# Output products on TensorE's row tiles, key work on its column tiles, and one pool of PSUM slots

## The chip, the cores and the metric

The kernel runs on one core of a Trainium2 chip. The metric is the device time of one execution in microseconds (us). Before the change three runs took 443.28, 443.36 and 443.82 us; the median is 443.36.

A core has five engines that work side by side, each through its own queue in order: TensorE (PE, matrix products into PSUM), VectorE (DVE), ScalarE (ACT), GpSimd (POOL) and SyncE (SP, which here only issues transfers). PSUM is the memory that TensorE writes; it has eight banks of 512 float32 columns by 128 partitions.

## The reference

Four batches of 12544 queries go through attention with 49 agents, and the result through a maxout network. With `sm` the softmax over the last axis of the scaled products:

```python
a2k = sm(agents, k)            # 49 x 12544 per batch
agent_v = a2k @ v              # 49 x 128
q2a = sm(q, agents)            # 12544 x 49
x = (q2a @ agent_v).reshape(50176, 128)
h = np.maximum(np.maximum(x @ w1, x @ w2), x @ w3)   # 768 wide
out = h @ w_out                # 50176 x 128, float32
```

## The kernel before

**The rearrangement.** x is never formed. For each batch the kernel multiplies agent_v with the weights once, into a small table G (49 rows used, in both halves of the partitions): its columns hold agent_v times w3-w1, times w2-w1, and times w1 times w_out. With e the exponentials of a query's 49 scores, the maximum over three becomes w1's part plus max(0 or u, v), where u comes from w3-w1 and v from w2-w1. So the output is e times G's linear part plus r times w_out, r being the maximum, all divided by the sum of e at the end.

**Blocks.** The queries are cut into 49 blocks `s` of 1024 (eight tiles of 128); block 48 takes the last 256 queries of each of the four batches. For each block:

- `ql`, `qc`: load by SP, cast to bf16 on POOL. Then the transpose: for 29 blocks by a transfer (`qd`), for 20 on TensorE (`qt`, L531) with a copy on DVE (`qe`, L535).
- `sc` (L541): scores, two matmuls of 512 columns, on column tiles (one gives partitions 0 to 63, the other 64 to 127). `ex` (L547): exponential on ACT. `su` (L553): four small matmuls for the sums; `re` (L558): reciprocals on DVE.
- For six slices `f` of the 768 hidden columns: `u` and `v` (L566), each a pair of matmuls with 49 rows and 512 columns, one on the upper, one on the lower 64 rows of the array (row tiles, which run side by side) into two banks. `a` (L579): ACT writes max(0, u); `x` (L582): DVE takes the maximum of that and v into r. For slice 4, v is added to u in place and ACT does both steps (L573, L576).
- In two halves of four query tiles, `o.s.0` and `o.s.1`: `li` (L595), the linear part with two matmuls of 256 columns each, then for each slice `p` (L604), four matmuls of 128 rows, 128 columns with r as the weights. `ov` (L611): DVE scales by the reciprocals. `st`: SP stores the block.

**Keys.** Batch 0's keys and values are worked through first, in 12 chunks (from 0 to about 39 us). Those of batches 1 to 3, in 11 chunks each, are spread over blocks 1 to 34: `ks` (scores, L367), `kx` (exponential), `kv` (values, L384), each nine small matmuls on the whole array with a host block's sums in the same PSUM tile; `va` on DVE and `ea` on POOL add up. When a batch is done, `gpa`, `gpc` and `gpl` make its G.

**Array modes.** A matmul runs on the whole array (full), on 64-row tiles (row) or on 64-column tiles (column). u and v are row, the query scores and G's products are column, all else is full.

**PSUM.** Three slots of two banks (`UV`) hold u, v and the products; two slots of one bank (`OM`) hold scores, sums and keys, transposed queries and the output halves: eight banks. `SLOTS` gives the counts.

**The order.** `graph` lists all operations with their engine and data; the costs, modes and service times it passes are not used when the kernel runs. The string `ORDER` then gives one sequence of all operations, with the slot of each new tile behind a slash; `Emit.run` issues them in it, and so each engine's queue has the order of its own operations in the string. An operation waits by semaphore for its data and for its slot's last reader.

Of the kernel before, what the change touches and what calls it, by code (L numbers as in the profile page):

```python
# [9 lines left out]
FP32 = mybir.dt.float32  # L10
# [7 lines left out]
DFF = NF * P  # L18
SCALE = 1.0 / math.sqrt(C)
C31, C21, C1O, WC = 0, DFF, 2 * DFF, 2 * DFF + 2 * C  # L20
# [11 lines left out]
SLOTS = {"UV": 3, "OM": 2, "LD": 13, "QB": 3, "KB": 3, "VB": 4, "KT": 3, "QT": 3, "EQ": 4, "EK": 4, "AS": 3,  # L32
         "R": 13, "RC": 4, "OS": 11, "G": 4, "VA": 2, "EA": 2, "ES": 2, "KR": 2}
SHAPE = {"UV": ([P, 2, 512], FP32), "OM": ([P, 512], FP32), "LD": ([P, KT, C], FP32), "QB": ([P, GT, C], BF16),
# [6 lines left out]
class Plan:  # L41
# [5 lines left out]
    def add(self, name, eng, fn, cost, mode=FULL, after=(), new=(), use=(), bank=None, serve=0.0):  # L47
# [4 lines left out]
        seq = [self.maker[t] for t in use if self.maker[t] not in after]  # L52
        self.ops.append(dict(name=name, eng=eng, fn=fn, pace=cost[0], lat=cost[1], mode=mode, after=list(after), seq=seq,
                             new=[t for _, t in new], use=[t for _, t in new] + list(use), bank=bank, serve=serve))
# [61 lines left out]
def graph(plan, em):  # L116
# [5 lines left out]
    for g, (t0, n) in enumerate(ch):  # L122
# [4 lines left out]
        add(f"kt0.{g}", PE, em.k_turn(g, n), mm(n, 128), after=[f"kc0.{g}", "prep"], new=[("UV", f"kT_ps0.{g}")], use=[f"kb0.{g}"])  # L127
        add(f"ke0.{g}", DVE, em.k_evacuate(g, n), dve_half(n * 128), after=[f"kt0.{g}"], new=[("KT", f"kT0.{g}")], use=[f"kT_ps0.{g}"])
        add(f"ks0.{g}", PE, em.k_scores(0, g, n, f"s0.{g}"), mm(n, 49), after=[f"ke0.{g}"], new=[("UV", f"s0.{g}")], use=[f"kT0.{g}"])
        add(f"kx0.{g}", ACT, em.k_exps(0, g, n, f"s0.{g}"), (n * 0.041 + 0.07, n * 0.041 + 0.2), after=[f"ks0.{g}"],  # L130
            new=[("EK", f"e0.{g}")], use=[f"s0.{g}"])
        add(f"to0.{g}", PE, em.totals(g, n), mm(1, n * 49), after=[f"kx0.{g}"], new=[("OM", "acc")] if g == 0 else [],
# [9 lines left out]
    for g in range(SPARE):  # L142
        add(f"wm.{g}", PE, em.warm(g), (0.2225, 0.45), new=[("OM" if g == 0 else "UV", f"warm.{g}")])
# [12 lines left out]
    add("tw1", PE, em.turn_w1, mm(NF, 128), after=["cw1", "prep"], new=[("OM", "tw1")])  # L156
# [6 lines left out]
    for name, c, d, eng in (("a", C31, ["d31a"], ACT), ("b", C31 + half, ["d31b", "d32"], DVE), ("c", C21, ["d21a"], ACT),  # L163
                            ("d", C21 + half, ["d21b"], DVE)):
        add(f"gp{name}", PE, em.product(0, c, c + half, f"gp{name}"), mm(1, half), mode=COL, after=["nr0"] + d, new=[("UV", f"gp{name}")])
        add(f"gv{name}", eng, em.product_out(0, c, c + half, c, f"gp{name}", eng), act(half) if eng == ACT else dve(half),
            after=[f"gp{name}"], use=[f"gp{name}", "G0"])
    add("pl", PE, em.prep_linear, mm(NF, 128), after=["ew1", "cwo"], new=[("OM", "pl")])
    add("el", ACT, em.evacuate_linear, (0.17, 0.31), after=["pl"], use=["pl"])
    add("gl", PE, em.product(0, C1O, WC, "gl"), mm(1, 256), mode=COL, after=["nr0", "el"], new=[("OM", "gl")])  # L170
# [713 lines left out]
```

## Time and profile before

| | |
|---|---|
| median of three runs | 443.36 us |
| span of the profiled execution, first to last instruction | 440.9 us |
| time of the profiled execution beyond its span | not in the page; the median is 2.46 us above the span |
| TensorE busy | 421.0 us (95%), 5246 matmuls |
| DVE busy | 390.6 us (89%) |
| ACT busy | 392.4 us (89%) |
| POOL busy | 169.3 us (38%) |
| u and v matmuls, L566 | 1248, 182.6 us busy |
| output matmuls, L604 to OM | 2340, 178.3 us busy |
| TensorE clock | 0.999 of full speed |

A group line gives: line, engine, operation, tiles out and in with their shapes, the count; busy time and the mean length of one in ns; then the engine's idle time just before these instructions and what ended it. A timeline line gives start, length, engine, line, operation and count of a merged run of equal instructions; PEld is TensorE loading weights. Matmuls overlap and their ends are modelled, so the spacing of starts says more than busy time. A window line gives the stretch, its length, then each engine's busy time with its count, the granted clock, the mean busy share of the 16 DMA engines and GB/s.

### The profile page before, as it was taken

How to read it: one execution, taken by the hardware profiler on the slowest of the kernel's cores; microseconds unless marked ns; L12 is line 12 of the kernel's file. 1: busy time of each engine (PE TensorE's matmuls, PEld its weight loads, DVE VectorE, ACT ScalarE, POOL GpSimd, SP SyncE). 2: the span in 40 equal slices, each digit the busy share in tenths (PEclk: the TensorE clock that was granted, in tenths of full speed). 3: DMA queues.
4: the chain of work that ended last, by engine and by line, in shares of the span. 5: the costliest groups of instructions: out<-in, count | busy, mean ns of one | idle time of the engine just before them, and what ended most of it. 6: DMA issues, size and time to landing. Idle time of an engine off the chain costs nothing.

```text
span 440.9 us, 12824 instructions
## 1 busy us (share of the span) xinstructions
PE 421.0 (95%) x5246; PEld 268.6 (61%) x5246; DVE 390.6 (89%) x495; ACT 392.4 (89%) x461; POOL 169.3 (38%) x176
## 2 busy tenths in 40 slices
PE   2678999999999999999999999999999999999997
PEld 2564565666666665666666666665665655656676
DVE  2236998999999999999999989989999999999996
ACT  2269999999998999999999999999999999999983
POOL 3541556667295413480746345634403102000000
PEclk9999999999999999999999999999999999999999
DMA  8999999999999999999999999999987952462144
GB/s 323 409 410 384 347 297 335 315 390 266 399 352 239 297 316 352 273 279 307 419 410 259 242 279 381 268 290 304 277 253 214 246 138 76 117 207 58 49 165 173
DMA packets 99157, 122.50 MB, mean 278 GB/s; under 512 B 72535, under 2 KB 75291, under 8 KB 99099
## 3 DMA queue, kind: packets, MB, share of 16 engines
q1 hardware_dynamic: 98752, 121.46, 92.2%
q8 instruction: 41, 0.67, 0.6%
q10 hardware_dynamic: 347, 0.23, 0.2%
q14 instruction: 17, 0.14, 0.1%
HBM read 78.74 MB, written 25.69 MB: 237 GB/s over the span
## 4 chain that ended last, share of the span: by engine, by line
PE 74%; DMA 15%; ACT 3%; POOL 3%; SPq 2%; DVE 1%; issue 1%; DVEq 0%; ACTq 0%; POOLq 0%
PE UV L566 31%; PE OM L604 28%; DMA LD<-in_k_dram 8%; PE OM L595 5%; PE OM L541 3%; DMA LD<-in_q_dram 2%; ACT AS L579 2%; DMA LD<-in_moe_w_dram 2%; DMA LD<-in_v_dram 2%; PE OM L384 2%; PE OM L531 2%; PE OM L367 2%; DMA KT<-KB 1%; SPq L333 1%; POOL KB L343 1%
## 5 line engine op out<-in xcount | busy, mean ns | idle before, releaser
L582 DVE TENSOR_TENSOR R<-UV,AS 128x1024 bf16<-128x1024 f32 x245 | 293.1, 1218 | 17.2 <-PE UV L566 13.2
L579 ACT ACTIVATE AS<-UV 128x1024 bf16<-128x1024 f32 x245 | 246.1, 1025 | 16.9 <-PE UV L566 13.3
L566 PE MATMUL UV<-EQ,G 49*128 49x512 bf16 (+1 forms) x1248 | 182.6, 369 | 1.0 <-DVE G L456 0.2
L604 PE MATMUL OM<-wo_bf,R 128*128 128x128 bf16 x2340 | 178.3, 220 | 0.0
L604 PEld LDWEIGHTS <-R 128*128 128x128 bf16 x2352 | 139.3, 98 | 41.1 <-issue 38.6
L566 PEld LDWEIGHTS <-G 49*128 49x128 bf16 x1248 | 60.4, 93 | 63.6 <-issue 23.3
L525 POOL CAST QB<-LD 128x1024 bf16<-128x1024 f32 x49 | 50.6, 1043 | 113.4 <-DMA LD<-in_q_dram 73.5
L611 DVE TENSOR_TENSOR OS<-OM,RC 128x512 f32<-128x512 f32 x98 | 66.8, 681 | 3.0 <-PE OM L604 2.0
L343 POOL CAST KB<-LD 128x1152 bf16<-128x1152 f32 (+2 forms) x45 | 50.0, 1120 | 48.7 <-DMA LD<-in_k_dram 32.0
L573 ACT ACTIVATE UV<-UV 128x1024 f32<-128x1024 f32 x49 | 49.9, 1018 | 2.6 <-PE UV L566 1.6
L576 ACT ACTIVATE R<-UV 128x1024 bf16<-128x1024 f32 x49 | 50.2, 1024 | 1.4 <-PE UV L566 0.6
L343 POOL CAST VB<-LD 128x1152 bf16<-128x1152 f32 (+1 forms) x33 | 37.5, 1141 | 26.2 <-PE OM L553 13.6
L595 PE MATMUL OM<-G,EQ 128*128 128x256 bf16 x195 | 37.8, 275 | 0.0
L482 POOL TENSOR_TENSOR EA<-EA,EK 128x441 f32<-128x441 f32 x27 | 27.7, 1026 | 19.1 <-ACT EK L373 18.4
L547 ACT ACTIVATE EQ<-OM 128x512 bf16<-128x512 f32 x49 | 29.5, 603 | 1.2 <-PE OM L541 1.1
L355 DVE COPY KT<-UV 128x1152 bf16<-128x1152 bf16 (+1 forms) x12 | 8.3, 701 | 15.8 <-PE UV L350 13.5
L595 PEld LDWEIGHTS <-EQ 128*128 128x128 bf16 x196 | 12.3, 97 | 15.7 <-issue 15.2
L341 ACT ACTIVATE VB<-LD 128x1152 bf16<-128x1152 f32 (+1 forms) x12 | 12.3, 1040 | 9.9 <-DMA LD<-in_v_dram 9.6
L367 PEld LDWEIGHTS <-KT 128*128 128x128 bf16 x392 | 14.6, 98 | 9.1 <-issue 5.1
L541 PE MATMUL OM<-QT,agT 128*64 128x512 bf16 (+1 forms) x104 | 19.9, 388 | 0.0
L384 PEld LDWEIGHTS <-VB 128*128 128x128 bf16 x392 | 14.0, 96 | 7.3 <-issue 5.6
L373 ACT ACTIVATE EK<-OM 128x441 bf16<-128x441 f32 (+1 forms) x33 | 18.0, 546 | 0.4 <-PE OM L553 0.3
(71 smaller groups left out, 193.3 us busy)
## 6 DMA issues: line engine op xcount, KB each, us to landing
LD<-in_q_dram SPq DMA_DIRECT2D x48, 512.0 KB, 6.8
out_dram<-OS SPq DMA_DIRECT2D x48, 512.0 KB, 5.1
LD<-in_k_dram SPq DMA_DIRECT2D x40, 576.0 KB, 8.3
LD<-in_v_dram SPq DMA_DIRECT2D x40, 576.0 KB, 9.7
LD<-in_v_dram SPq DMA_DIRECT2D x3, 512.0 KB, 8.0
LD<-in_k_dram SPq DMA_DIRECT2D x3, 512.0 KB, 11.2
LD<-in_moe_w_dram SPq DMA_DIRECT2D x6, 192.0 KB, 8.6
KT<-KB SPq DMA_TRANSPOSE x33, 6.6
```

The costliest lines, as they stand in the source:

```text
L343: (self.nc.gpsimd if eng == POOL else self.nc.vector).tensor_copy(out=out, in_=src)
L525: return lambda: self.nc.gpsimd.tensor_copy(out=self.t[f"qb.{s}"], in_=self.t[f"q.{s}"][:, :GT, :])
L541: self.nc.tensor.matmul(self.t[f"qs.{s}"][h * H:(h + 1) * H, jj * P:(jj + pairs) * P], self.agT[:, b, :], self.t[f"qT.{s}"][:, 2 * jj + h: ...
L547: return lambda: self.nc.scalar.activation(self.t[f"e.{s}"], self.t[f"qs.{s}"], AF.Exp, scale=SCALE)
L566: self.nc.tensor.matmul(t[:, h, jj * P:(jj + pairs) * P], self.t[f"G{b}"][h * H:h * H + A, c + f * P:c + (f + 1) * P], self.t[f"e.{s}"][h ...
L573: return lambda: self.nc.scalar.activation(self.t[f"u.{s}.{f}"], self.t[f"u.{s}.{f}"], AF.Relu)
L576: return lambda: self.nc.scalar.activation(self.t[f"r.{s}.{f}"], self.t[f"u.{s}.{f}"], AF.Relu)
L579: return lambda: self.nc.scalar.activation(self.t[f"a.{s}.{f}"], self.t[f"u.{s}.{f}"], AF.Relu)
L582: return lambda: self.nc.vector.tensor_tensor(out=self.t[f"r.{s}.{f}"], in0=self.t[f"v.{s}.{f}"], in1=self.t[f"a.{s}.{f}"], op=ALU.max)
L595: self.nc.tensor.matmul(out[:, c:c + 2 * C], self.t[f"e.{s}"][:, j // 2 * P:(j // 2 + 1) * P], self.t[f"G{of[j // 2]}"][:, C1O:C1O + 2 * C ...
L604: self.nc.tensor.matmul(out[:, c:c + C], self.t[f"r.{s}.{f}"][:, j % 2, j // 2 * P:(j // 2 + 1) * P], self.wo_bf[:, f, :], start=False, st ...
L611: self.nc.vector.tensor_tensor(out=self.t[f"os.{s}"][:, j:j + n, :], in0=self.flat(f"o.{s}.{o}")[:, :n * C].rearrange("p (j c) -> p j c", ...
```

## The change

- **Output products.** A block's output is one tile `o` of two banks (bank 0 for the first four query tiles, bank 1 for the last four) in place of two halves. Each slice's product is split over the 128 rows of r and w_out: `p` takes, for each of four positions, rows 0 to 63 into bank 0 and rows 64 to 127 into bank 1, as a row-tile pair; `y` takes the other rows for each bank. So the two row tiles never add to one bank within a step, but p and y use the banks the other way round. Where the order goes from one side to the other on an unfinished `o`, `turns` marks the operation and a TensorE drain is issued ahead of it.
- **The linear step** is four row-tile pairs of 128 columns; G's linear part is 128 columns wide instead of 256.
- **The transposes on TensorE** are eight row-tile pairs of 64 columns, and the DVE copy reads and writes them in runs of 64.
- **Keys of batches 1 to 3 and all sums** run on column tiles: each matmul of 128 weight columns becomes a pair of 64.
- **PSUM.** One pool `PP` of four slots of two banks holds everything. A block's scores (bank 0) and its sums with the hosted keys (bank 1) share one tile `ax`.
- **The scaling** is one DVE operation of 1024 columns, in the last block two times two of 256. The last block's store cuts the tile as slices of query tiles four apart.
- **The order** is new for all operations.

```diff
-SLOTS = {"UV": 3, "OM": 2, "LD": 13, "QB": 3, "KB": 3, "VB": 4, "KT": 3, "QT": 3, "EQ": 4, "EK": 4, "AS": 3,
+SLOTS = {"PP": 4, "LD": 13, "QB": 3, "KB": 3, "VB": 4, "KT": 3, "QT": 3, "EQ": 4, "EK": 4, "AS": 3,
          "R": 13, "RC": 4, "OS": 11, "G": 4, "VA": 2, "EA": 2, "ES": 2, "KR": 2}
...
+    def turns(self, order):
+
+        turned, side = set(), {}
+        for n in order:
+            o = self.ops[self.index[n]]
+            if o["side"]:
+                t = o["new"][0] if o["new"] else o["use"][-1]
+                if side.get(t, o["side"]) != o["side"]:
+                    turned.add(n)
+                    side = {}
+                side[t] = o["side"]
+        return turned
...
+            if name in turned:
+                self.nc.tensor.drain()
             o["fn"]()
...
+    def later_scores(self, b, g, n, m):
+        def fn():
+            t = self.keys(b, m)
+            for j in range(n):
+                for h, r in self.halves():
+                    self.mm(t[r, j * A:(j + 1) * A], self.t[f"kT{b}.{g}"][:, j, r], self.agT[:, b, :A], start=(j == 0), stop=True)
+        return fn
...
     def q_turn(self, s):
         def fn():
-            t = self.half(f"qT_ps.{s}")
+            t = self.t[f"qT_ps.{s}"].bitcast(BF16)
             for j in range(GT):
-                self.nc.tensor.transpose(t[:, j * P:(j + 1) * P], self.t[f"qb.{s}"][:, j, :], self.ident)
+                for h, r in self.halves():
+                    self.nc.tensor.transpose(t[:, h, j * H:(j + 1) * H], self.t[f"qb.{s}"][r, j, :], self.ident[r, r])
         return fn
...
+            t, e = self.t[f"ax.{s}"], self.t[f"e.{s}"]
             for jj in range(GT // 2):
-                c = CS + 2 * jj
-                self.nc.tensor.matmul(self.t[m][:, c:c + 2], self.t[f"e.{s}"][:, jj * P:(jj + 1) * P], self.sel,
-                                      start=(first and jj == 0), stop=True, skip_group_check=True)
...
+                for h, r in self.halves():
+                    self.mm(t[r, 1, CS + 2 * jj:CS + 2 * jj + 2], e[:, jj * P + h * H:jj * P + (h + 1) * H], self.sel, start=(lone and jj == 0),
+                            stop=True)
+        return fn
...
+    def out_linear(self, s):
         def fn():
             of = [p[0] for p in parts_of(s) for _ in range(p[4])]
...
+            for jj in range(GT // 2):
+                x = slice(jj * P, (jj + 1) * P)
+                for h in range(2):
+                    r = slice(h * H, h * H + A)
+                    self.mm(self.t[f"o.{s}"][:, h, x], self.t[f"e.{s}"][r, x], self.t[f"G{of[jj]}"][r, C1O:WC], start=(jj == 0), stop=False)
+        return fn
+
+    def out_hidden(self, s, f, side):
+
+        def fn():
+            for jj in range(GT // 2):
+                x = slice(jj * P, (jj + 1) * P)
+                for h, r in self.halves():
+                    i = h if side == 1 else 1 - h
+                    self.mm(self.t[f"o.{s}"][:, i, x], self.t[f"r.{s}.{f}"][r, i, x], self.wo_bf[r, f, :], start=False, stop=True)
+        return fn
+
+    def out_scale(self, s):
+        return lambda: self.nc.vector.tensor_tensor(
+            out=self.t[f"os.{s}"], in0=self.flat(f"o.{s}").rearrange("p (j c) -> p j c", c=C),
+            in1=self.t[f"rc.{s}"].unsqueeze(2).to_broadcast([P, GT, C]), op=ALU.mult)
```

Two blocks of the order, before and after, around the output products (a word is an operation, the number behind the slash its slot):

```diff
-p.40.0.2 ov.40.0/4 v.41.4 x.41.4/0 qc.48/0
-v.41.5/1 u.42.1/0 a.42.1/2 x.41.5/6 sc.43/1 ex.43/0 li.40.1/0 p.40.1.4 v.42.0/2 x.42.0/10 p.40.1.0 u.41.3/1 a.41.3/1 v.42.1/0
...
+re.41/2 x.40.2/4 v.40.5/3 u.41.0/0 a.41.0/1 x.40.5/7 li.40/1 p.40.3 p.40.1
+u.41.2/2 a.41.2/2 p.40.0 v.41.0/0 x.41.0/8 p.40.2 qc.44/2 qd.44/0 p.40.4 u.41.1/3 a.41.1/0 p.40.5 u.41.4/2 a.41.4 y.40.2 y.40.0
+v.41.1/0 x.41.1/2 u.41.3/3 a.41.3/1 y.40.1 y.40.5 y.40.3 y.40.4 ov.40/1
...
```

More of the change, by code (lines that the diff above doesn't have):

```diff
@@ L45, in __init__, with add @@
         self.ops, self.index, self.tiles, self.maker = [], {}, {}, {}
-    def add(self, name, eng, fn, cost, mode=FULL, after=(), new=(), use=(), bank=None, serve=0.0):
+    def add(self, name, eng, fn, cost, mode=FULL, after=(), new=(), use=(), bank=None, serve=0.0, side=0):
         self.index[name] = len(self.ops)
@@ L51, in add, with close @@
             self.maker[t] = name
-        seq = [self.maker[t] for t in use if self.maker[t] not in after]
-        self.ops.append(dict(name=name, eng=eng, fn=fn, pace=cost[0], lat=cost[1], mode=mode, after=list(after), seq=seq,
-                             new=[t for _, t in new], use=[t for _, t in new] + list(use), bank=bank, serve=serve))
+        self.ops.append(dict(name=name, eng=eng, fn=fn, pace=cost[0], lat=cost[1], mode=mode, after=list(after),
+                             new=[t for _, t in new], use=[t for _, t in new] + list(use), bank=bank, serve=serve, side=side))
+    def close(self):
+        for o in self.ops:
+            o["seq"] = [self.maker[t] for t in o["use"] if t not in o["new"] and self.maker[t] not in o["after"]]
+    def turns(self, order):
[9 more added lines that the diff above has]
+        return turned
     def places(self, order, given):
@@ L650 @@
     graph(plan, em)
+    plan.close()
     order, given = [], {}
```

630 lines of the change are left out of this document (303 added, 327 removed).

## The prediction

> **What bounds the kernel now.** I read the page first, then the windows, the waits, and last TensorE's timeline, where single groups of matmuls can be timed against each other.
>
> ```profile
> span 440.9 us, 12824 instructions
> ...
> PE 421.0 (95%) x5246; PEld 268.6 (61%) x5246; DVE 390.6 (89%) x495; ACT 392.4 (89%) x461; POOL 169.3 (38%) x176
> ...
> PE 74%; DMA 15%; ACT 3%; POOL 3%; SPq 2%; DVE 1%; issue 1%; DVEq 0%; ACTq 0%; POOLq 0%
> ...
> L582 DVE TENSOR_TENSOR R<-UV,AS 128x1024 bf16<-128x1024 f32 x245 | 293.1, 1218 | 17.2 <-PE UV L566 13.2
> ...
> L604 PE MATMUL OM<-wo_bf,R 128*128 128x128 bf16 x2340 | 178.3, 220 | 0.0
> L604 PEld LDWEIGHTS <-R 128*128 128x128 bf16 x2352 | 139.3, 98 | 41.1 <-issue 38.6
> ```
>
> The runs' median, 443.36, is 2.46 us above this span; I take that as what lies around the span, and every change below as a change of the span. The chain is TensorE's (74%), and L604 has no idle before it at all. From 39 us on, where the blocks start:
>
> ```profile
> core 0: us, PE busy (x) PEld busy (x) DVE busy (x) ACT busy (x) POOL busy (x), PEclk, DMA share, GB/s
> 39.00:441.00 402.00, 397.21 (x4915) 250.81 (x4913) 377.85 (x463) 373.81 (x435) 155.02 (x157) 1.00 0.93 268
> ```
>
> Per block of 49 that is 8.2 us, with DVE idle 24 us and ACT 28 us in total. They mostly wait for TensorE, briefly:
>
> ```profile
> ACT AS L579 <- PE UV L566: 13.3, 42, 0.6
> DVE R L582 <- PE UV L566: 13.2, 35, 0.7
> ```
>
> So TensorE bounds, with two engines close behind. What fills it is seen in starts, not in the modelled ends:
>
> ```profile
> 249.73 0.60 PE L566 MATMUL UV<-EQ,G 49*128 49x512 bf16 x4
> 250.26 0.84 PE L604 MATMUL OM<-wo_bf,R 128*128 128x128 bf16 x12
> 250.94 0.38 PE L595 MATMUL OM<-G,EQ 128*128 128x256 bf16 x2
> 251.25 0.60 PE L566 MATMUL UV<-EQ,G 49*128 49x512 bf16 x4
> 251.79 0.40 PE L604 MATMUL OM<-wo_bf,R 128*128 128x128 bf16 x4
> ...
> 387.92 0.61 PE L566 MATMUL UV<-EQ,G 49*128 49x512 bf16 x4
> 388.46 0.41 PE L541 MATMUL OM<-QT,agT 128*64 128x512 bf16 x2
> 388.80 0.39 PE L566 MATMUL UV<-EQ,G 49*128 49x512 bf16 x2
> ```
>
> Twelve full-array matmuls take 250.26 to 250.94: 0.68, or 0.057 each. Two row-tile pairs of 512 columns record 0.60 and one pair 0.39, so a pair takes 0.215; yet from 249.73 the next form starts after 0.53, not 0.43. The 0.10 is a change of array mode, row tiles to full. Back, 250.94 to 251.25, two 256-column matmuls (0.107 each by the same pace) leave 0.10 again. Into and out of column tiles it is 0.11 (387.92 to 388.46) and 0.12 (388.46 to 388.80).
>
> **The change: modes.** Going along the order's TensorE operations with their modes, I count 592 changes before: 480 between row and full, 70 between row and column, 42 between full and column. At 0.10, 0.115 and 0.10 that is 60 us. After it are 234: 219 row to column or back, 15 with full-array work, all in the start. That is 26.7 us. Gain 33.5 us.
>
> **Output products.** One p step of four 128x128 matmuls becomes p and y, each four pairs of 64-row halves. The nearest row is the last block, which already runs 128-column row-tile pairs with new weights each:
>
> ```profile
> 432.05 0.84 PE L566 MATMUL UV<-EQ,G 49*128 49x128 bf16 x24
> 432.82 1.07 PE L604 MATMUL OM<-wo_bf,R 128*128 128x128 bf16 x16
> 433.82 0.64 PE L566 MATMUL UV<-EQ,G 49*128 49x128 bf16 x16
> ```
>
> Twelve pairs take 0.77 less a mode change of 0.10: 0.056 a pair, as the full matmul. So 48 pairs for 48 matmuls a block, no cost. The linear step drops from four 256-column matmuls (0.43) to four pairs (0.224): 49 x 0.205 = 10 us gained. [...]
>
> **Drains.** The order gives 105: each time p and y alternate on an unfinished o. No row shows one. It can hardly cost less than a mode change, 0.10; from above, a 128-column matmul's record outlasts its pace by 0.220 - 0.057 = 0.163, and a load nobody hides adds 0.098: 0.26. I take the middle, 0.18, being nearest to waiting out the record: 18.9 us (10.5 to 27.3).
>
> **Column tiles and query transposes.** Nearest rows: narrow full-array matmuls, the full-array transposes, and the last block's column pairs.
>
> ```profile
> 30.84 0.63 PE L384 MATMUL OM<-EK,VB 128*128 128x49 bf16 x18
> 31.31 0.38 PE L367 MATMUL UV<-agT,KT 128*128 128x49 bf16 x9
> ...
> 232.18 0.62 PE L531 MATMUL OM<-ident,QB 128*128 128x128 bf16 x8
> 232.63 0.61 PE L604 MATMUL OM<-wo_bf,R 128*128 128x128 bf16 x8
> ...
> 420.24 0.41 PE L541 MATMUL OM<-QT,agT 128*64 128x128 bf16 x8
> 420.59 0.64 PE L566 MATMUL UV<-EQ,G 49*128 49x512 bf16 x4
> ...
> L566 PEld LDWEIGHTS <-G 49*128 49x128 bf16 x1248 | 60.4, 93 | 63.6 <-issue 23.3 <-DVE G L456 0.4 <-DVE R L582 0.2
> ...
> L541 PEld LDWEIGHTS <-agT 128*64 128x64 bf16 x104 | 5.8, 106 | 9.1 <-issue 6.3 <-DMA out_dram<-OS 0.3
> ```
>
> A narrow full matmul takes 0.47/18 = 0.026; a column pair with new weights at most (0.35 - 0.12)/4 = 0.057, and that row streams 128 columns, so it is a ceiling. I take 0.040, midway. Keys: 33 chunks x 2 steps x 9 pairs x (0.040 - 0.025) = 8.9 us (0 to 18.7). Sums: 49 x (4 x 0.040 - 0.10) = 2.9 us (0 to 6.2). The 20 transposes of query blocks: 0.45 each before, eight pairs of 64 columns after, 0.20 to 0.45; at 0.25 they gain 4 us (0 to 5). [...]
>
> **TensorE's sum:** -33.5 - 10 - 4 + 18.9 + 8.9 + 2.9 = -16.8 us. All best ends: -38; all worst: +8.7.
>
> **What is late next.** DVE:
>
> ```profile
> 382.54 2.36 DVE L582 TENSOR_TENSOR R<-UV,AS 128x1024 bf16<-128x1024 f32 x2 [0.30 <-PE UV L566]
> ...
> 388.03 0.69 DVE L611 TENSOR_TENSOR OS<-OM,RC 128x512 f32<-128x512 f32 x1
> 388.64 5.02 DVE L582 TENSOR_TENSOR R<-UV,AS 128x1024 bf16<-128x1024 f32 x4
> ```
>
> A maximum takes 2.36 - 1.22 = 1.14, an output scaling of 512 columns 0.61. One scaling of 1024 at a maximum's pace saves 0.08 a block, 4 us: 374 us of work in the 402. But the pool is smaller: u and v had three slots of their own; now four serve u, v, a whole o (held from the linear step through twelve steps and the 1.14 scaling) and ax (scores to sums and keys). In 33 places, against 9, the next DVE operation reads a product that can only start in the slot this operation frees, 17 of them x.s.0, v.s.1, x.s.1. Each leaves DVE idle for a TensorE round trip; the 0.39 of a pair's record with a little queueing makes 0.5: 16 us. 374 + 16 = 390, 12 us under 402. That is less gain than TensorE's 16.8, so DVE decides: 443.4 - 12 = **431 us**. ACT (373.81) stays behind. SP keeps its 260 issues (loads, transposes, stores) and POOL its 161 operations; only their order moves, and they run ahead of TensorE. Each drain holds everything queued behind it on TensorE, the next u and v among it, so ACT and DVE feel it too once they are the bound. The 20 copies of transposed queries now write runs of 64 columns:
>
> ```profile
> L535 DVE COPY QT<-OM 128x1024 bf16<-128x1024 bf16 x20 | 13.6, 682 | 3.4 <-PE OM L531 3.4
> ```
>
> I take their time as unchanged, since the runs stay long; at the pace of a float maximum they would take 20 x (1.22 - 0.68) = 11 us more on DVE. In the last block two half scalings in four instructions follow the last product where one of 0.42 did: +0.9, against some 1.5 us of TensorE work no longer after the last maximum; nothing net. The first blocks wait for the same 31 loads as before: nothing.
>
> **Rivals.**
> 1. The round trips hide and TensorE's cheaper ends hold: DVE's 374 alone bounds, 443.4 - 28 + a few waits = 420. For it: DVE's other waits were short (0.4). Against: three engines within a few per cent. 0.10.
> 2. Slower by the pool. Of PSUM tiles that follow a DVE or ACT reader, 140 of 694 now wait for the latest instruction listed on that engine, before 58 of 792; those with two or more to spare fall from 290 to 63. At each extra one TensorE can wait up to an instruction, 1.0 to 1.2. It decides from 16.8/82 = 0.2 us a place; at 0.25, 447; at 0.4, 459. Against it: TensorE would then have time to wait. 0.27, of which slower 0.19.
> 3. Drains and column loads at their upper ends: +8.7, 452. 0.15, slower 0.12.
> 4. The halves do not run at 0.056 over long bursts: the x24 row is only 48 instructions with their loads, and TensorE now gets twice the output matmuls. If loads were not overlapped the pair would take the load's 0.098: 49 x 48 x 0.042 = 99 us, 525. [...] Against: that row. 0.04.
> 5. Transfers hold the middle back:
>
> ```profile
> POOL QB L525 <- DMA LD<-in_q_dram: 73.5, 13, 18.9
> ...
> 20.00:40.00 20.00, 16.24 (x256) 11.85 (x254) 8.48 (x17) 14.94 (x21) 5.50 (x5) 1.00 1.03 401
> ...
> 240.00:320.00 80.00, 79.83 (x1016) 50.75 (x1012) 74.13 (x94) 77.02 (x91) 38.38 (x40) 1.00 1.12 291
> ```
>
> The share is as high at 240 to 320 as in the load-bound start. Then only the last 12 blocks gain, 0.25 each: 440. Against: TensorE waits for none of it now. 0.06.
>
> **How the numbers follow.** Forecast 431 (own range 424 to 440): 0.38. Faster: 0.38 + 0.10 + 0.05 (rival 2 mild) + 0.02 (3) + 0.05 (5) = 0.60. Slower: 0.19 + 0.12 + 0.04 = 0.35. Within 0.2%, what a measurement here can tell from no change: 0.05. The range 418 to 455 leaves out rival 4 and the tails of 1, 2 and 3, some 0.15.
>
> **What would show it.** Right: p and y pairs 0.056 apart; mode changes only around column work; gaps of about 0.18 between p and y; key groups of nine pairs lasting 0.36; DVE idle growing around v.s.1 with TensorE idle no longer zero. Wrong: TensorE waits on slots of tenths of a us at most acquisitions, drains over 0.3, output pairs slower than 0.06, or DMA waits ahead of key scores.

## The result, and the profile after

The changed kernel takes 512.25 us (median; 510.32 to 512.82 in four runs) against 443.32 before: a ratio of 1.155, with a 95% interval of 1.1525 to 1.1573. The prediction said 431, with a range up to 455. Both the sign and the size were wrong. Single runs of kernels of after's kind differ by up to 2.5%, the longer ones mostly with a lower mean clock (in e14 below 476.48 us at 0.945 and 488.13 at 0.923); where that matters the range is given.

The page of after answers to the lines shown of before: span, busy times, the granted clock in tenths over 40 slices, the instruction queue (packets, MB, share), the chain, then the costliest groups (busy, mean ns of one, idle before and what ended it).

```profile
span 511.0 us, 19885 instructions
...
PE 430.3 (84%) x8738; PEld 285.9 (56%) x8738; DVE 390.4 (76%) x447; ACT 399.3 (78%) x461; POOL 169.7 (33%) x176
...
PEclk9976799979799999899999999997988999999999
...
q8 instruction: 68, 1.11, 0.9%
...
PE 11%; DVE 5%; ACT 2%; issue 2%; DMA 1%; SPq 0%; DVEq 0%; ACTq 0%
...
L620 DVE TENSOR_TENSOR R<-PP,AS 128x1024 bf16<-128x1024 f32 x245 | 292.8, 1217 | 59.5 <-PE PP L336 49.2
L617 ACT ACTIVATE AS<-PP 128x1024 bf16<-128x1024 f32 x245 | 245.5, 1025 | 56.4 <-PE PP L336 50.2
L336 PE MATMUL PP<-EQ,G 49*128 49x512 bf16 (+1 forms) x1248 | 216.8, 384 | 14.8 <-DVE OS L644 3.5
L336 PE MATMUL PP<-wo_bf,R 64*128 64x128 bf16 x4704 | 205.2, 220 | 15.0 <-issue 4.8
```

All three main engines got idler: TensorE's share fell from 95% to 84%, DVE's and ACT's from 89% to 76 and 78%. DVE's and ACT's idle is a wait for TensorE (49.2 and 50.2 us, before 13.2 and 13.3). So TensorE still sets the pace, and it stands still more. The chain was followed back for 21% of the span only, so it does not help here. The clock, flat before, has dips, and the instruction queue carried 68 packets (of 16 KB each) where before it carried 41. The two lines of before:

```profile
PEclk9999999999999999999999999999999999999999
...
q8 instruction: 41, 0.67, 0.6%
```

The same stretch as in the prediction, from 39 us to the end:

```profile
39.00:511.00 472.00, 406.96 (x8427) 268.97 (x8422) 379.83 (x420) 382.47 (x438) 155.55 (x157) 0.95 0.82 229
```

**What TensorE's time went on.** I booked each gap from one matmul's start to the next: first the streaming at the paces of the prediction's rows (0.056 for 128 columns, 0.215 for 512), then up to 0.11 at a change of mode, up to 0.26 at a drain, the extra streaming time where the granted clock is 0.5, a rest over 0.4 us where the next matmul waits for no semaphore ("stall"), and what is left as a wait. In us, from 39 us to the last matmul of the profiled execution, for before, after and six of the experiments below (in brackets their labels). Each column is one execution. Behind before they took 512.8, 504.0, 503.3, 523.7, 498.9, 466.5 and 492.1 us, which is not always near the median of the kernel's runs:

| | before | after | key scores first (e1) | no drains (e2) | full-array products (e3) | ACT and DVE halved (e5) | halved, three edits (e13) | other order (e11) |
|---|---|---|---|---|---|---|---|---|
| streaming and rests under 0.05 | 331 | 322 | 321 | 320 | 322 | 321 | 321 | 323 |
| mode changes | 58 | 24 | 23 | 24 | 86 | 23 | 23 | 24 |
| drains | 0 | 26.5 | 26 | 0 | 0 | 26.5 | 0 | 21 |
| semaphore waits | 9 | 56 | 50 | 67 | 50 | 42 | 30 | 46 |
| stalls without a semaphore | 0 | 19 | 17 | 14 | 3 | 22 | 29 | 20 |
| half clock | 0 | 19 | 20 | 31 | 15 | 17 | 17 | 11 |
| sum | 398 | 466 | 457 | 456 | 477 | 452 | 419 | 445 |

The first three rows are the work that the prediction summed for TensorE: -8.8, -34.6 and +26.5, together -17. It had said -16.8. The loss is in the other three, which were 9 us before and are 94 after.

Rows of TensorE's timeline show each kind:

```profile
70.23 0.41 PE L336 MATMUL PP<-QT,agT 128*64 128x512 bf16 x2
71.33 0.47 PE L336 MATMUL PP<-agT,KT 128*64 128x49 bf16 x18 [0.69 <-ACT EQ L582]
71.73 0.60 PE L336 MATMUL PP<-EQ,G 49*128 49x512 bf16 x4
...
100.24 0.46 PE L336 MATMUL PP<-agT,KT 128*64 128x49 bf16 x17
101.89 0.21 PE L336 MATMUL PP<-agT,KT 128*64 128x49 bf16 x1 [1.18 <-issue]
...
129.18 0.39 PE L564 MATMUL PP<-ident,QB 64*128 64x64 bf16 x15
131.74 0.19 PE L564 MATMUL PP<-ident,QB 64*128 64x64 bf16 x1 [2.16 <-issue]
131.74 0.40 PE L336 MATMUL PP<-EQ,G 49*128 49x512 bf16 x2
131.97 0.40 PE L336 MATMUL PP<-wo_bf,R 64*128 64x128 bf16 x8
132.19 0.39 PE L336 MATMUL PP<-EQ,G 49*128 49x512 bf16 x2
...
240.32 0.62 PE L336 MATMUL PP<-wo_bf,R 64*128 64x128 bf16 x16
240.78 0.81 PE L336 MATMUL PP<-EQ,G 49*128 49x512 bf16 x6
...
400.62 0.88 PE L336 MATMUL PP<-wo_bf,R 64*128 64x128 bf16 x16
401.33 0.60 PE L336 MATMUL PP<-EQ,G 49*128 49x512 bf16 x4
```

- **The pairs.** Four pairs from 131.97 to 132.19 are 0.22: 0.056 a pair, as predicted.
- **A drain** holds TensorE's next instruction back until the work ahead of it has ended (in e4 below the next load starts 0.08 us behind the last matmul's record). Eight pairs without one take 240.32 to 240.78, 0.46; with one, 400.62 to 401.33, 0.71. A drain costs 0.25 there.
- **The shared tile.** At 71.33 the key scores wait for the exponential of ACT, though it reads bank 0 of the tile `ax` and they write bank 1: here the wait goes by tile, not by bank. In 14 of the 33 chunks the order puts key scores behind that exponential.
- **A stall.** The sixteenth of 16 query transposes starts 2.56 us after the run of fifteen began, and waits for nothing that the profile shows ("issue"). The trace's record of the instruction queue has a transfer of 16 KB that starts at 129.3, 2.4 us before it goes on. There are 13 such stalls over 0.5 us, and each ends 2.3 to 2.7 us after the start of such a transfer. Counted along all of TensorE's instructions in the trace, 12 of the 13 stand at the same place of every 256 (the 193rd to 195th), where one block of instructions ends and the next has not come. At 101.89 one stands in front of the last of 18 key matmuls.

From 39 us to the last blocks six stretches have half the clock, 48 us in all. Two behind stalls and the one at the start of the blocks (columns as in the prediction's window lines; the granted clock is the figure behind POOL's):

```profile
102.80:109.60 6.80, 6.69 (x93) 4.12 (x94) 4.16 (x6) 4.82 (x6) 3.31 (x3) 0.50 1.03 411
133.50:140.30 6.80, 6.80 (x106) 4.38 (x102) 4.62 (x7) 4.57 (x6) 3.09 (x3) 0.50 0.95 347
41.30:58.40 17.10, 16.35 (x150) 7.61 (x152) 11.94 (x19) 13.69 (x19) 9.09 (x9) 0.50 1.01 298
```

TensorE's longer waits by what ended them (us in total, times, longest). This view counts only idle time of over 0.15 us behind the modelled ends of matmuls, so its totals are smaller than the table's:

```profile
PE PP L336 <- ACT EQ L582: 13.9, 24, 1.1
PE PP L336 <- issue: 13.4, 14, 3.1
...
PE PP L336 <- DVE OS L644: 3.5, 10, 0.5
PE PP L336 <- ACT AS L617: 3.2, 7, 1.0
PE PP L336 <- ACT R L614: 3.1, 9, 0.5
PE PP L336 <- DVE R L620: 2.7, 8, 0.5
```

Going through TensorE's operations one by one, 20.6 us of the waits are key scores, key values and sums behind the exponential in the shared tile. Some 31 us are u, v, the linear step and scores that wait for a slot: for the maximum on DVE 13, the scaling 9, the first step on ACT 6. Before, slot waits were 7 us.

### The profile page after: what moved, and what is told of

The parts are those of the page before. It is cut to its first block, busy times and chain, and to the rows that moved or that the text cites. A ratio compares the mean times of both kernels' runs of the same rounds, so it can differ in the third digit from the quotient of the medians.

```text
span 511.0 us, 19885 instructions
## 1 busy us (share of the span) xinstructions
PE 430.3 (84%) x8738; PEld 285.9 (56%) x8738; DVE 390.4 (76%) x447; ACT 399.3 (78%) x461; POOL 169.7 (33%) x176
## 5 line engine op out<-in xcount | busy, mean ns | idle before, releaser
L620 DVE TENSOR_TENSOR R<-PP,AS 128x1024 bf16<-128x1024 f32 x245 | 292.8, 1217 | 59.5 <-PE PP L336 49.2
L617 ACT ACTIVATE AS<-PP 128x1024 bf16<-128x1024 f32 x245 | 245.5, 1025 | 56.4 <-PE PP L336 50.2
L336 PE MATMUL PP<-EQ,G 49*128 49x512 bf16 (+1 forms) x1248 | 216.8, 384 | 14.8 <-DVE OS L644 3.5
L336 PE MATMUL PP<-wo_bf,R 64*128 64x128 bf16 x4704 | 205.2, 220 | 15.0 <-issue 4.8
L336 PEld LDWEIGHTS <-R 64*128 64x128 bf16 x4704 | 162.0, 96 | 71.1 <-issue 45.6
L362 POOL CAST KB<-LD 128x1152 bf16<-128x1152 f32 (+2 forms) x45 | 49.9, 1116 | 81.9 <-DMA KT<-KB 33.5
L644 DVE TENSOR_TENSOR OS<-PP,RC 128x1024 f32<-128x1024 f32 x48 | 58.5, 1218 | 2.6 <-PE PP L336 1.7
L611 ACT ACTIVATE PP<-PP 128x1024 f32<-128x1024 f32 x49 | 49.7, 1015 | 4.2 <-PE PP L336 4.0
L614 ACT ACTIVATE R<-PP 128x1024 bf16<-128x1024 f32 x49 | 50.3, 1026 | 1.7 <-PE PP L336 1.4
L336 PEld LDWEIGHTS <-EQ 49*128 49x128 bf16 (+1 forms) x784 | 27.6, 106 | 31.2 <-issue 17.0
L582 ACT ACTIVATE EQ<-PP 128x512 bf16<-128x512 f32 x49 | 29.3, 598 | 9.7 <-PE PP L336 9.6
L336 PE MATMUL PP<-agT,KT 128*64 128x49 bf16 (+1 forms) x686 | 21.1, 194 | 13.3 <-ACT EQ L582 9.6
L336 PE MATMUL PP<-sel,EQ 128*64 128x2 bf16 x392 | 15.0, 175 | 10.7 <-issue 7.2
```

The costliest lines, as they stand in the source:

```text
L336: self.nc.tensor.matmul(*args, skip_group_check=True, **kw)
L362: (self.nc.gpsimd if eng == POOL else self.nc.vector).tensor_copy(out=out, in_=src)
L582: return lambda: self.nc.scalar.activation(self.t[f"e.{s}"], self.t[f"ax.{s}"][:, 0, :], AF.Exp, scale=SCALE)
L611: return lambda: self.nc.scalar.activation(self.t[f"u.{s}.{f}"], self.t[f"u.{s}.{f}"], AF.Relu)
L614: return lambda: self.nc.scalar.activation(self.t[f"r.{s}.{f}"], self.t[f"u.{s}.{f}"], AF.Relu)
L617: return lambda: self.nc.scalar.activation(self.t[f"a.{s}.{f}"], self.t[f"u.{s}.{f}"], AF.Relu)
```

## The experiments

From the traces I had five theories for the 69 us: T1, the drains; T2, the half clock; T3, the shared tile; T4, the supply of instructions, of which TensorE now needs 17476 (matmuls and loads) in place of 10492; T5, the four slots and the new order, whose round trips leave TensorE waiting. All ran beside the kernel before, at 443.0 to 443.6.

### One stop taken out of after

**e1_ks_first.** In the order, 14 times like this:

```diff
- sc.3/3 ex.3/1 kt1.2/0 ks1.2 kx1.2/1
+ sc.3/3 kt1.2/0 ks1.2 ex.3/1 kx1.2/1
```

> The kernel after, with one edit to the order: for 14 of the 33 key chunks the key scores stood behind the exponential of the block's scores, and now stand between the scores and that exponential (as in the other 19 chunks). Both use the one tile ax in different banks. Theory T3 (the shared tile makes the key scores wait for the exponential, though their banks differ): in the trace of after TensorE stands about 0.88 us from the end of the scores to the key scores at these places, 11.8 us in all; so 512 falls by 10 to 14 us, to 498 to 502, and by up to 10 more if stalls that dropped the clock go. Against it, the exponential then waits for the key scores, 0.28 us at 14 places, 4 us on ACT. Rival (TensorE's waits only move to the next slot, since ACT or DVE set the pace): 508 to 512.

Measured: 508.56 us (504.04 to 512.10). The key scores no longer wait; in the trace of this run they follow the scores at once:

```profile
236.81 0.41 PE L336 MATMUL PP<-QT,agT 128*64 128x512 bf16 x2
237.05 0.44 PE L336 MATMUL PP<-agT,KT 128*64 128x49 bf16 x18
```

Of 11.8 us that they had waited, 3.7 came off the median and 0 to 8 off single runs; the 10 to 14 of T3 were not reached. In this trace, of the shortest run, the waits of u and v for the maximum's slots grew from 12.4 to 14.2 us, the sums' stayed. The wait is real, but it is not what decides.

**e2_one_side.**

```diff
-                    i = h if side == 1 else 1 - h
+                    i = h
```

> The kernel after with both output steps on the same side (rows 0 to 63 into bank 0, rows 64 to 127 into bank 1), so that no TensorE drain is issued; the same number of matmuls, loads and the same order. It leaves out the crossed half of every product and adds the straight half twice. Theory T1 (drains cost what stands between the matmuls, 105 times 0.24 to 0.27, on the path): 512 falls by 26 to 28 us, to 484 to 486. Rival a (TensorE waits for slots anyway, so a drain's time is spent as a wait for a slot): falls by under 12. Rival b (each drain also holds back the next u and v, so that ACT and DVE lose as well): falls by over 35.

Measured: 498.60 us (496.55 to 503.25), 13.7 less. That is half of T1's 26 to 28 and just over rival a's 12. The table points to why: 26.5 us of drains went, and 11 us of waits and 12 of half clock came. Its trace is of the longest run, with the lowest clock (0.924), so the share of the half clock is that run's.

**e7_warm_late.** The ten `wm` are moved in the order to between `to0.4` and `nr0`.

> The kernel after with its ten warm-up matmuls, which the new order puts into the first 10 us, moved to between the last key steps of batch 0 and the first u of block 0 (36 to 41 us), as the order before has them. Theory T2 (the half clock from 41.3 to 58.4 us comes from the gaps just ahead of it, which the warm-up no longer fills): clock 1.0 in 41 to 58 us, and since TensorE is busy for most of that stretch, 6 to 9 us less: 503 to 506. Its mean clock rises from 0.945 to about 0.97. Rival (ACT and DVE set the pace of the first blocks, or the clock drops from another cause): within 2 us of 512.

Measured: 510.15 us (508.07 to 512.62). The half clock from 41.3 to 58.4 shrank to 53.6 to 57.0, and the time fell by 2, as the rival had it. The ninth maximum ends 1.7 us earlier than in after (61.3 against 63.0), so the first blocks are hardly paced by the clock. Further on other stretches came: from 39 us to the last blocks 41 us of half clock in all, where after has 48.

**e8_three.** These three edits together.

> Three edits of the earlier runs together: key scores ahead of the exponential, both output steps on one side (no drains; the crossed half of each product left out, the straight half twice), and the warm-up just ahead of block 0. One by one they gave -3.7, -13.7 and -2.1 us. If each loss is met by another wait only because the others are still there (theory T5: what is left is the round trip through the four slots), they add to no more: 490 to 496. If they hide one another: 465 to 480, towards the 61 us that drains, the shared tile and the first half-clock stretch take up in the trace of after.

Measured: 494.39 us; three runs 494 to 495, one 484.52, whose mean clock was 0.979 against 0.948 to 0.962. The median is in the first range expected, the shortest run between the two. One by one the edits gave 19.4 us, together 18, in the shortest run 28, of the 61 named above. What is taken out is largely made up by waits elsewhere: TensorE's semaphore waits in the trace, of a run of 494.31, are 63 us, more than in after.

### Parts of the change, alone on before

**e4_before_drains.**

```diff
+            if name in DRAINED:          # 105 of the output steps
+                self.nc.tensor.drain()
             o["fn"]()
```

> The kernel before with a TensorE drain ahead of 105 of its output steps, each following another output step, some two in each block: one part of the change alone. Theory T1 (a drain costs what stood between the matmuls in the trace of after, 0.24 to 0.27, where TensorE sets the pace): 443.5 + 25 to 28 = 469 to 472. The 0.18 of the prediction gives 462. Rival (TensorE has slack that takes the drains up): under 455.

Measured: 467.54 us (467.22 to 467.74), +24.5, or 0.234 a drain. Twelve output matmuls with one and without, up to the start of the next form:

```profile
249.74 1.10 PE L606 MATMUL OM<-wo_bf,R 128*128 128x128 bf16 x12
250.77 0.82 PE L568 MATMUL UV<-EQ,G 49*128 49x512 bf16 x6
...
253.63 0.84 PE L606 MATMUL OM<-wo_bf,R 128*128 128x128 bf16 x12
254.40 0.41 PE L543 MATMUL OM<-QT,agT 128*64 128x512 bf16 x2
```

1.03 against 0.77. That is close under T1's 469 to 472: T1 holds where TensorE has no slack.

**e6_before_columns.** `k_scores` and `values` of batches 1 to 3 and `sums` as pairs, for example:

```diff
-                self.nc.tensor.matmul(self.t[m][:, c:c + 2], self.t[f"e.{s}"][:, jj * P:(jj + 1) * P], self.sel,
+                for r in (slice(0, H), slice(H, P)):
+                    self.nc.tensor.matmul(self.t[m][r, c:c + 2], self.t[f"e.{s}"][:, jj * P + r.start:jj * P + r.stop], self.sel,
```

> The kernel before with the keys of batches 1 to 3 and all sums on column tiles: one part of the change alone. In this order that makes 706 array mode changes of 592, +114 at 0.10 to 0.115 = +11 to 13. The pairs by the trace of after (nine pairs of a key step in 0.28 to 0.30 where nine full matmuls took 0.24): 66 steps at 0.05 = +3.3; sums +2 to 3. Together 460 to 463. By the prediction's 0.040 a pair: +12 + 8.9 + 2.9, 467.

Measured: 457.84 us (457.14 to 458.68), +14.8, a little under both forecasts. By the table's bookkeeping 10.7 of it are the added mode changes and 6.4 the pairs; the prediction had 11.8 for the pairs. In after, where nearly all other work is on row tiles, a key step takes 0.40 (71.33 to 71.73 in the rows above) with its mode change of 0.11: 0.29, not 0.36.

**e10_before_cut.** Nothing of the change, only more instructions:

```diff
-            for b, _, n, jj, pairs in parts_of(s):
+            for b, jj in [(p[0], p[3] + i) for p in parts_of(s) for i in range(p[4])]:
                 for h in range(2):
-                    self.nc.tensor.matmul(t[:, h, jj * P:(jj + pairs) * P],
+                    self.nc.tensor.matmul(t[:, h, jj * P:(jj + 1) * P],
```

> The kernel before with each u and v pair of 512 columns cut into four pairs of 128 columns (as its last block has them): 3528 more matmuls and as many loads, so 8774 of each, almost the 8738 of after; no drains, no column work, the old order and slots. By the paces of the trace (four pairs of 128 in 0.224 for one of 512 in 0.215) 588 x 0.009 = 5 us: 448. Theory T4 (TensorE's instructions come in blocks by transfers, and when twice as many are needed the next block comes too late): about 68 fetches in place of 41, stalls of 0.5 to 3 us inside operations that wait for no semaphore, some 10 to 20 us in all, and half-clock stretches after some of them: 458 to 475. Rival (the stalls in after come from something else in it, the drains or the slots): 446 to 450, no such stalls.

Measured: 458.22 us (456.63 to 461.48), +15. Its page has 68 packets on the instruction queue:

```profile
PE 426.9 (94%) x8702; PEld 344.8 (76%) x8702; DVE 392.1 (86%) x495; ACT 393.8 (86%) x461; POOL 169.7 (37%) x176
...
q8 instruction: 68, 1.11, 1.0%
```

and its timeline has the stall, in a kernel with the old order, the old slots and no drain:

```profile
91.15 0.53 PE L566 MATMUL UV<-EQ,G 49*128 49x128 bf16 x10
94.41 0.50 PE L566 MATMUL UV<-EQ,G 49*128 49x128 bf16 x6 [2.74 <-issue]
```

Seven stalls over 0.5 us with 7.8 us, and one stretch of half clock, 94.3 to 97.7. The kernel before has none of either. T4 is shown: more instructions bring the stalls, with nothing else of the change. Stalls and half clock account for some 9 of these 15 us; the narrower pairs take 6 (325.5 against 319.4 for the streaming without the small rests).

The number is not all of it. After has as many instructions and twice the time in stalls, and all 20 stalls (13 and seven) lie before 356 us, although TensorE is as fast behind 400 us in after, at 17.5 matmuls per us (the last figure but one is the busy share of the DMA engines):

```profile
80.00:160.00 80.00, 66.04 (x1400) 43.90 (x1399) 60.48 (x70) 58.90 (x70) 39.42 (x41) 0.91 1.05 306
...
400.00:511.00 111.00, 95.88 (x1944) 63.85 (x1943) 95.61 (x96) 95.11 (x104) 7.28 (x7) 0.99 0.39 117
```

What differs is the load of the DMA engines (1.05 against 0.39), and when the transfer of the next block of 256 instructions starts. In after, up to 355 us, it starts 3.4 us (median, at most 7.3) after TensorE has begun a block, and a block lasts 6.8; behind 365 us it starts 0.7 us (at most 2.1) after. In before, over the same stretch, it starts 2.5 us (at most 4.3) after, but a block lasts at least 8.5. So the late start and the 2.4 us from there on outlast a block only where blocks are short. That the other transfers make the start late is not shown: no run changed them alone, and behind 400 us there are no keys and no transposes on TensorE either.

### The output products, the readers, the order

**e3_full_products.**

```diff
-                for h, r in self.halves():
-                    i = h if side == 1 else 1 - h
-                    self.mm(self.t[f"o.{s}"][:, i, x], self.t[f"r.{s}.{f}"][r, i, x], self.wo_bf[r, f, :], start=False, stop=True)
+                i = side - 1
+                self.mm(self.t[f"o.{s}"][:, i, x], self.t[f"r.{s}.{f}"][:, i, x], self.wo_bf[:, f, :], start=False, stop=True)
```

> The kernel after with the output products on the whole array as before: p is four matmuls of 128 rows into bank 0, y four into bank 1. No drains, 2352 matmuls and 2352 loads fewer, and array mode changes 873 instead of 234 in this order. If the change's loss lies in the halves: drains -27, the stalls at instruction fetches -14 (68 fetches fall to about 50), against 639 more mode changes at 0.10, +64; by TensorE's sum alone 512 + 23 = 535. Theory T5 (the pool of four slots and the order cost the time, about 31 us of waits for slots, and TensorE's own work hides in these waits): 505 to 515, with the waits of u and v on slots falling as mode changes take their place. Theory T4 (instruction supply): the mid-operation stalls over 0.5 us, 11 in after with 14 to 15 us, fall to 2 or fewer and with them the half clock after 100 us; then 24 + 14 less: 497 to 505.

Measured: 523.73 us (522.11 to 524.30). None of the three expected it: in this order 873 mode changes cost 62 us more, no drain and almost no stall (3 us) is left, and the waits are 50, against 56 in after. With 50 packets on the instruction queue no stall is left at the end of a block, as T4 says. The waits do not come from the halves: they stand in the order and the slots, and they hide little, since the time went up.

**e5_after_light and e9_before_light.** ACT and DVE work half of the columns, in after and in before; W is 256.

```diff
-        return lambda: self.nc.scalar.activation(self.t[f"a.{s}.{f}"], self.t[f"u.{s}.{f}"], AF.Relu)
+        return lambda: self.nc.scalar.activation(self.t[f"a.{s}.{f}"][:, :, :W], self.t[f"u.{s}.{f}"][:, :, :W], AF.Relu)
```

> The kernel after, with ACT and DVE working only the first 256 of each 512 columns of u and v, and the output products reading that half of r twice: half of the maxout's work is left out, all of TensorE's matmuls, loads and drains and the order stay. It shows what TensorE needs alone. Theory T5 (TensorE waits for ACT and DVE to give slots of the small pool back): the waits over 0.4 us, 112 with 53 us in after, fall to under 15 us, and the time to 440 to 465, the stalls at instruction fetches (about 15 us) and the drains (26) staying. Rival (the waits are chains through the keys, POOL or transfers): stays over 490.

> The kernel before with the same cut (half of the maxout's work on ACT and DVE left out, TensorE's work unchanged): the control. TensorE sets its pace already, with 13 waits over 0.4 us (4 us): 443.5 falls by 4 to 14, to 430 to 440. With the run beside it: TensorE's own work in after against before. The prediction's sum of -16.8 for TensorE with drains at 0.25 in place of 0.18 (+7) and fetch stalls (+15) would put the two within 10 us of each other; if after's is over 20 us above, TensorE's own work was misjudged as well.

Measured: 497.12 us (493.19 to 499.01) and 436.65 (435.60 to 437.51). Before falls by 6.4, as a kernel that TensorE paces. After falls by 15 only, and stands 60 us above its control. The time lies where the rival said, over 490, and T5 in this form falls: the slots that ACT and DVE hold too long account for some 15 us (the waits for the maximum and the first step nearly vanish, the total of waits goes from 56 to 42). The rest of what the table has over before is drains, stalls, half clock, and waits for the exponential (17.6) and the scaling (11), which this edit leaves about as they were.

**e13_light_three.** The three edits of e8 on that.

> Three edits (key scores ahead of the exponential, both output steps on one side and so no drains, warm-up just ahead of block 0) on the kernel after with ACT and DVE working half of u's and v's columns. Half of the maxout's work and the crossed half of the products are left out; all matmuls stay. With full work these three edits gave 18 us (512 to 494), 44 less than they take up in the trace of after, since other waits came in their place. If those others are waits for slots that ACT and DVE still hold: here the drains (26.5) and the key scores' waits (9.5 in the run with half the work) go for good, 497 - 36 = 461, or less where the clock stays up, and waits fall from 42 to under 28 us. If TensorE's remaining waits do not hang on ACT and DVE at all: 479, the same 18 off 497.

Measured: 467.39 us (466.48 to 468.56), 30 less, between the two. The drains go for good and the waits fall to 30, but the stalls rise to 29:

```profile
PE PP L337 <- issue: 22.9, 20, 2.6
...
PE PP L337 <- DVE OS L645: 5.6, 20, 0.5
PE PP L337 <- ACT EQ L583: 4.4, 15, 0.7
```

Before's control needs 437 with the same cut. With no drain left, after still needs 30 us more. By the table it has 29 us of stalls, 30 of waits and 17 of half clock, while its mode changes and streaming are 45 us below before's. The stalls are the most of any run in the table, 29 us against 22 in e5 and 19 in after; that they grow because TensorE goes faster is argued, and e2, faster than after too, has only 14.

**e11_after_order, e14_light_order and e12_before_order.** The same operations as after (and, for e12, as before) in another order that was searched for with the durations of the traces. A piece of after's order and of e11's:

```diff
- ov.23/2 sc.25/2 ks3.1 kx3.1/1 v.24.3/0 ex.25/1 v.24.4 x.24.3/2 kv3.1 su.25
+ ov.23/3 a.24.4 ea3.0/0 sc.25/1 ks3.1 kx3.1/3 ea3.1 kl3.10/12 v.24.3/0 x.24.3/8 st.20 v.24.4 u.24.5/3 kt3.4/0 ex.25/1 su.25
```

> The kernel after, operation for operation, in another order and other slots, found by moving operations in the order so as to shorten TensorE's waits with the durations of the traces: 83 drains in place of 105, 237 mode changes, key scores mostly not behind the exponential. If the loss lies in the order that came with the change: waits over 0.4 us fall from 112 with 53 us to under 35 us; drains -5.5; the fetch stalls (68 fetches, some 16 us) and half-clock stretches stay: 485 to 498. If it lies in the four slots as such: no gain over 8 us, 504 to 512. In no case below the 443 of before, since the fetch stalls and the drains left (20 us) stay.

> The kernel after in the other order (83 drains; 489.5 with full work), with ACT and DVE working half of u's and v's columns; half of the maxout's work is left out. It asks what the four slots still cost in an order that fits them better. If ACT's and DVE's hold on the slots makes the 46 us of waits there: they fall to under 20 us and the time to 460 to 468. If it is as in the first order (13 us of 56 went): 475 to 479.

> The kernel before, operation for operation, in another order and other slots found in the same way; 584 mode changes in place of 592. TensorE's idle of about 17 us in the middle (waits for u's and v's slots, three waits for transposed keys) shrinks by some 7 to 9 us: 434 to 438, which would beat both kernels. Rival (the transfers do not come as early as assumed in the new order): 443 to 450.

Measured: e11 489.48 us (485.23 to 492.08), so 23 of the 69 us are the order's; the half clock shrank as well, to 11 us. e14 483.29 (476.48 to 488.13): with half of ACT's and DVE's work the waits fall from 46 to 27, yet the time by 6 in the median; stalls (21) and half clock (19) are not below e11's. Its two shorter runs, 476.48 and 479.18 at a mean clock of 0.945, are 12 below e11 and at the second of its two cases (475 to 479); the other two, at 0.923 and 0.934, are at neither. e12 453.30 (451.95 to 453.96), 2.3% above before and outside both of its ranges: its TensorE waits more, not less (15 us), and its granted clock is 0.75 in the first 40 us and 0.86 in the next 40, where before's is 1.00. Why was not followed up. No version with the whole work beat the kernel before.

## Why the prediction was wrong

Point by point, in its own steps:

- **Modes**, -33.5: measured -34.6. Right.
- **Output products**, 0: right, 0.056 a pair over the whole run. Rival 4, which had them slower, did not happen.
- **Linear step, transposes, keys, sums**, -10 - 4 + 8.9 + 2.9 = -2.2: measured -8.8 for streaming and small rests together. Part of the difference is e6's: the column pairs cost 6.4 us more than full matmuls there, where the prediction had 11.8; in after such a pair takes 0.032, not 0.040.
- **Drains**, +18.9 (up to 27.3): 26.5 in the trace, 24.5 alone on before. The range held, the middle did not. As the prediction had it, a drain waits out the last matmul's record: in e4 that record ends at 250.14, the next load starts 0.08 later and the next matmul 0.01 behind the load. So the second term of the upper end, a load of 0.098 that nobody hides, is not what the trace shows; with 0.163 for the record the two gaps make 0.25.
- **TensorE's sum**, -16.8: -17. Right by luck: the drains were 7.6 too low and the small work 6.6 too high, and these errors cancel.
- **What is late next: "so DVE decides"**. This is the step that failed. It compared the sum of TensorE's work, 402 less 16.8, with DVE's 390 and took the larger, and so gave TensorE's own standing still no place: the 82 slot waits that the prediction counted stood in a rival only, and stalls and half clock nowhere. DVE's work did not grow (377.85 busy before, 379.83 after, in the stretch from 39 us). TensorE, with 17 us less to do, lost 85 us more: 47 to semaphore waits, 19 to stalls, 19 to half clock. DVE then waits for TensorE 79 times with 49.2 us, 0.62 each, where the prediction had 33 round trips at 0.5.
- **Rival 2, the pool**, named the right place for a part. At its upper price, 0.4 at 82 more places, it has 33 us; slot waits grew by 24. Its time, 459 at most, is 53 short, because it knew neither the shared tile (20.6), nor the stalls, nor the clock. What was said against it, that TensorE would then have time to wait, was the mistake itself: an engine that has less work does not get its waits for free when its work and its waits stand one behind the other in its queue.
- **The `ax` tile.** The change's text said that scores and keys share a tile. The prediction read it as fewer slots and did not ask which operations now wait for each other.
- **Instructions.** It counted "48 pairs for 48 matmuls a block, no cost", but a pair is two matmuls and two loads. No term stood for their supply, and no rival: rival 4 had the loads slower, not the instructions late. Its bounds could not show it: nothing in before's profile waits for instructions, with 41 packets on that queue.
- **Rival 1** had the round trips hidden; DVE's waits for TensorE rose instead. **Rival 3, drains and loads at their upper ends**: the drains were there, the loads were not. **Rival 5, transfers**: in after the profile puts none of TensorE's waits down to a transfer of data; those that it stood still for were of its instructions.
- Of the signs named beforehand, "TensorE waits on slots of tenths of a us at most acquisitions" came in part: 206 semaphore waits of 0.27 each on average, of which slots are some 31 of 56 us. Drains over 0.3, slower pairs and transfer waits did not come.

**What is shown and what stays open.** Shown by runs: the cost of a drain (e4), the stalls as an effect of the number of instructions (e10, e3; not why a block's transfer starts late), the wait in the shared tile and its removal (e1), 23 us of the order (e11), and that a shorter hold of the slots by ACT and DVE gives 15 us and no more in after's order (e5). The parts do not add: each stop taken out lets another grow. Open is what the half clock costs by itself. e7 took most of its longest stretch out for 2 us, and no run held the clock up with all else the same. Open too is how good an order four slots allow; e11 is one better order, not the best.

## What to carry to other kernels

Sum an engine's work and its stops, not only its work: waits, drains, stalls and mode changes stand one behind another in the queue of an engine that works in order, and "the larger of two engines' busy sums" is a lower bound (here TensorE had 17 us less to do and lost 85 more). When matmuls are halved, count TensorE's instructions (loads too) per us, look at the instruction queue's packets, and compare the time that a block of instructions lasts with the time until the next one has come (in after 6.8 us, against a transfer that started up to 7.3 us into the block and 2.4 from there on). When two uses are put into one tile, list what now waits for what, even where the banks differ (here 20.6 us of waits).

## What the runs showed of the hardware

- **Instruction blocks.** 68 packets for 17476 matmuls and loads, 41 for 10492: one for every 256 or 257. A stall ends 2.2 to 2.7 us after its block's transfer starts (after and e10). In after, up to 355 us, a block lasts 6.8 us (median; the shortest 4.4), and the transfer of the next starts up to 7.3 us after TensorE has begun it. In before, where over the same stretch a block lasts at least 8.5 us and the transfer starts at most 4.3 us into it, no block shows a stall; with 68 packets the stalls are 19 us in after and, those over 0.5 us, 7.8 in e10. The most in the table is 29, in e13.
- **The clock.** Half-clock stretches in after last 3.4, 6.8 or 17.1 us, and two of them began behind gaps of 1.18 us (at 101.89 in after, with a wait of 0.69 just behind it) and of 2.16 (at 131.74). Stalls of 1.93 and 1.51 us at 187 and 202 in the same trace were followed by no drop. The stretch from 379.3 has no stall ahead of it at all, only three semaphore waits of 0.44, 0.69 and 0.30 us in the 3.5 us before it. So no length of gap that brings the half clock is shown.
- **A drain** of TensorE costs 0.23 to 0.26 us between matmuls that otherwise follow without a gap: 0.234 over the 105 of e4, 0.26 in e4's two rows (1.03 against 0.77), 0.25 in after (0.71 against 0.46).
